# Squares of the state powers on either of two engines, and a new written-out order of 1808 steps

## The chip, the cores and the metric

One core of one Trainium2 chip runs the whole kernel. The metric is device time in microseconds (us), as the median of several executions. The core has five engines that run at the same time, each with its own queue of instructions, taken strictly in the order in which the program puts them: TensorE (PE in the profile, its weight loads PEld), VectorE (DVE), ScalarE (ACT), GpSimd (POOL) and SyncE (SP), which here issues all DMAs. An instruction that must wait for another engine's result holds up everything behind it on its own engine.

## The reference, cut to what matters

```python
a = _A_ref(x, wq, wk, wv, wo, beta)      # attention in 4 segments of 512 tokens, 32 heads of 16, with a memory
    logits = einsum('bhqd,bhkd->bhqk', qs, ks) * scale + mask ; p = softmax(logits)
    o = g * (pq @ M) / (pq @ z + 1e-6) + (1 - g) * (p @ vs)      # M, z: summed over the segments before
b = _B_ref(u, A_re, A_im, B_re, B_im, C_re, C_im, log_dt, Dskip) # state-space convolution, u = x
    P = exp(dt * A * l)                  # for all l < 2048: powers of one complex number for each (d, n)
    K = einsum('dn,dnl,dn->dl', C, P, dt * B).real
    y = irfft(rfft(u) * rfft(K))[:L] + u * Dskip
return g * a + (1 - g) * b               # g = sigmoid(x . gate_w)
```

x is 2048 x 512 in bf16. The powers exp(dt A l) are made by squaring: from Z, squared nine times, come the 1st, 2nd, 4th, ... 512th power.

## The kernel before, in words

The program is written as a graph of 1808 steps (`build_graph`). A step is one DMA, one instruction of ACT, DVE or POOL, or a group of matmuls. Its parts, with the tags used in the texts below:

- **State powers** (`ssm_prep`, `ssm_powers`; tags prep, pow, pwc; lines 840 to 866). For each half h of 256 channels x states and each k < 9: a square of Z on ACT (line 850, 128 x 512 floats, real and imaginary part at once), the difference of its halves on DVE (851), and the product 2 Re Im on DVE (852); they are the next Z. A cast of Z to bf16 (858 on ACT, 859 on DVE), a negated copy (862) and a small DMA make the form that the tables use. In `pow0.2`, 0 is the half and 2 the k.
- **Tables** (`tables`, tags tabc, tab, lag; lines 1316 to 1404). For each of four channel groups DVE multiplies powers into two tables (lines 1346, 1349, 1355, 1358); tabc are the copies of 256 elements that begin a table, either engine may do them. PE makes the convolution's kernel from the tables (lag), and an eviction brings it from PSUM.
- **Attention** (`project`, `scores`, `ophase`; tags pk, pq, sc, mk, pv, nrm, mem, oT). For each segment s and head group hg, `sc s.hg.X` are the scores on PE and then the exponential on ACT (lines 1190 and 1237, 128 x 2048), pv the product with the values, nrm the normalisation on DVE (lines 1151, 1152, 1154), oT the transposition of the result. oT3.3 is the last.
- **Convolution** (`conv`; tags X, E, K, Y, V). X, E and K are products on PE with evictions (line 229 on ACT, 230 on DVE), Y is DVE's product (1487), V the inverse product on PE, its eviction, and a DMA of 128 KB that scatters the rows of V into V2. CD is the load of the constants that K and V use.
- **Finals** (`finals`; lines 1503 to 1559). For each of 16 output blocks PE adds up: `fin` (three head groups; for blocks 8 to 15 also the skip term), `fir` (first half of V2), `fih` (the last head group, needs oT of all four segments), `fis` (second half of V2, so it needs every scatter of V16 to V31). Blocks 8 to 15 stay in PSUM ("held") and out is one eviction with a scale (232 on ACT, 233 on DVE). Blocks 0 to 7 are spilled: xD (1521) and spl (1543) on DVE before fih, out (1557) on DVE after fis.

What sets the order: `ORDER` (line 375) is a text with one word for each step, in one global order. In `1036v/0` 1036 is the number of the step in the graph, `v` puts a step that either engine may do on DVE (`a` on ACT; other steps have no letter that counts), and the numbers behind `/` are the buffers or PSUM banks that its tiles take. `replay` (in the class `Sched`) deals the words out to the engines' queues, so each engine's order is the global order cut to its own steps; `emit` puts a semaphore wait before a step for every producer, and for the last users of the buffer or bank that it takes. Nothing is decided at run time. SP's queue, which holds 257 DMAs, is such an order too: a DMA whose data is not there yet stops all DMAs behind it. `evac` (line 227 on) makes an eviction or copy that either engine may do:

```python
return self.op("ANY", 0.0, None, r=r, w=w, pw=pw, key=key,
               alts={"ACT": (("As" if sb else "A", n, scale is not None), fa),
                     "DVE": ((("V4" if sb is True else sb) if sb else "V2" if psum16 else "V1", n), fd)})
```

Of the kernel before, what the change touches and what calls it, by code (L numbers as in the profile page):

```python
# [7 lines left out]
ACT = mybir.ActivationFunctionType  # L8
# [355 lines left out]
PW, PWS = (1.0, 8.0), 0.6  # L364
# [11 lines left out]
9/0 0/0 15/0 16/0 10/1 66/0 29/0 32/0/0 38/1/0 39 33v 41/0 48/1 30/2 31a 40/2 13/2 12/3 47/3 11/4 17/3 43/4 50/5 42/6  # L376
49/7 54/0 44 3/0 51 45 46 56/8 18 19 52 53 215/0 67/4 69/5 55/9 59/0 57/10 58 34/0/1 61/11 70v/0 60/12 64/0 68v 62/13
71/0 72/1 27/0 14/5 36/6/2 74a/0 73 75 24/0 218/1 63 23/0 266/2/0/0 35a 186/2 220/0 85/3 83/1 84 1236/1 26/0 222/7 37a
189/2 7/0 76 1244/5/0 181/4 1249/4/1 77/3 95/0 22/0 199/0 78/5 96/6 97 103/1 626/0 182/3 86v/1 1/0 184/0 841/0 79 221a
87 88 106a/2 1242/0 219a 1243a 1245a 104/7 105 115/1 185/0 206/6 107 117/0 91/1 2/0 116 207/0 1246 118a/3 210/1/1/1  # L380
211a 187/0 212 129/4 1247/0 65 6/0 108 20 127/1 200 128 119 190 1248a 399/0 5/0 183 267a 1036v/0 98v/4 142v/5 213/1/0
141/6 214a 120 21 139/1 223a 228/0/0/0 1252/2/0 201 229 627/5 628 208/0 1253a 1257/0 140 1040v/0 1039v 1250a 216/3
217a 224 268 1044 225 1037v 1251 1038v 230 842/1 843 130v/6 271/2/1/1 413/1 256/0/0 1042/0 257 1045 151/2 152/7 1254/3
131 1041 153 132 258 231 311/0/2/2 143 1043 89/3 272 233/0/1 234 165/2 227 188 235 1255a 226 154v/7 269/1/1 238/0/2
239 1049 166v/8 312a 144 202/0 1050 270a 155 90 8/0 1237/3/1 156 1046 273 236/0 240 1239/1 1240a 237 241 99/1 1238a
1256 167 242/0/3 168 203/0 243 244 274 1051 1263/2/0 1264a 1047/0 1052 1265/1 101/3 1266a 163/2 357/3/2 287/0/1 288
1053 245 209/0 1048 100 246 1241 416/2 1278/1 289 417a 247/1 1056/0 358a 232/1/0 275 1054 276/0 250/0/3 251 252 400/2
401 1268/3/1 248 164 1270/1 249/0 175a/9 314/2/0 315a 253/0 254 1269a 283/0/3 284 1061 255 259 1055 1271a 1267 4/0 285
1260/2/0 1261a 1272 1258/3 176 177 1057 1259a 278/0/2 279 280 1062 1262 260 261/2 1273/1/1 1275/2 1276a 313 354/3/3/1
355a 316/2/0/0 1274a 1277 1063 301/0/0 1058 262 302 317 1059/0 281/3 263 264 303 403/0 1286/1/0 1287a 282 286 290 402  # L390
291 359/0/1/1 1060 360 319 318 1065 1066/0 295/0/2 292/3 1294/2/1 1295a 296 297 28/0 1067 320/1 361 1296/2 362 363
1068 1069/0 338/0/1 339 1299/0 293 1064 191/0 109/0 1070 1297a 364 1298 192/0 340 1071/2/0 1075/1 1076 1077 204 111/4
110 121/3 294/1 1079/0 1080 1081a 123/0 1072 1078a 205 1073 1074a 1083/0 1086v/0 1088a 1284/3 1285a 1090v/0 122 298/0
356 1087v 299 300 1094 1092/0 1089v 1095 136a/4 330/0/2 331 332 1085 135/6 112v/2 1091 304 1288 133/1 1279/1/1 472/2/1
473a 113 114 1093 305 321/0/3 1099 306/4 1084 1096 322 323 134 145/2 1100 1097/0 1082 405/3/1/0 406a 341/2 342 307
344/0/0 345 1281/3 346 1101 1280a 476/0 308 309 1098 1282a 1283 1102 420/0 1106/0 421a 326/0/1 327 426/1/0/0 146/7 328
1103 1307/3/0 427 1308a 147 157/0 324/0 325 366/0/3 367 368 343 1105 428 408/3/0 1104 80a/0 329 1107 333 334 335/5
1108 375/0/1 376 347 160a/3 377 348 1109/0 349/0 418/1 371/0/2 372 419a 409a 1111 124a/1 373 1110 469/1/0/2 1302/3/1
412/1 470a 383/0/0 384 1303a 1115 336 1116/0 369/1 370 374 337/0 81 125 385 1117 126 1112 1300/0 1301a 265/0 1305/3
1306a 378 379 389/0/3 137 390 158/2 159 386/0 82 1118 350 1119/0 380/1 1304 351 352 414/3 404/1 387 391 102v/6 161  # L400
477/2/1/1 92a/5 407 431/0/1 432 415a 381 388 423 425 422 172a/8 1113 382/1 392 393 1309 1120 1114 162 433 93 645/3/0
424 471 478 440/0/0 441 394/2 646a 479 429 94 1121/1/0 171/3 1129/3 1122 169/3 1123 277 395 1130 442 138 1125/2 1131a
353 148a/9 1126 1127 365 448/0/2 396 1128a 449 480 450 430/0/1 1312/3/1 173 1313a 1124a 174 1140v/0 481 1136v/0
522/2/2/1 1144 1138v 170 1145 1137v 1139v 454/0/3 523a 434/3 1149 1142/0 482 455 456 149 150 576/0/2 1133 1310/1 451/2
178a/7 452 1135 435 1141 1311a 1314 577a 436/0/2 437 438 647/1 1150 648a 1143 1151 1147/0 1146 410/0 1289/0/0 1290a
489/0/1 490 1152 1148 179 180 439 453 310 1317/1/1 1291/0 1155 491 493/0/2 1336/0 494 1292a 1156/0 1315/0 1318a 1153
495 457 458 1316a 397 690/1/3/0 691a 484/0/3 485 1157 1348/1 1154 486 1159/0 1132 1134 525/0/0 526a 1158 1161 411
459/3 443 530/1/0/0 444 445/4 531 1160 532 501/0/0 446 502 503 487/0 1166/0 1165 1340/2 488 492 524 1337/1/0 1167 1341
447/0 507/0/3 1397/3 1162 508 1168 474/1 1342a 460 1163 504/3 505 506 573/1/1/2 461 1169/0 496 1164 509 552/0/0 553
574a 581/1/1/1 497 510 554 511 635/2/1 844 1293 1319 1321/0 1345/1 1320/0 1350/4/0 636a 1170 462/3/5/0 512/0 398 498/1  # L410
845 1171/5/0 463 582 637/0 1175/2 1176 1351a 1177 1178a 1172 1173 513 464 583 514/1 475 1333/2 1174a 1324/4 533 465
1334/1/1 1335a 515/1/2/1 499 558/0/1 640 527/1 575 516 559 1401/0 560 529/1 517 500 195/0 1179/1 1180 629 1322/0/2 528
1181a 518 1190v/0 1447/1 466 584 1187v/0 566/1/4/0 535/0/2 536 567 1352/2 534/1 1194 1188v 585 568 1195 569 1369/2 586
1199 1323a 537 1346/0 1347a 1186v 555/2 519 544/0/3 1189a 545 546 643/3 1200 538/1 1191 467 644a 1185 539 1201 520
521/0 1192/0 630 1202 556 698/0/0/0 699 540/0/2 541 542 1193 700 1197/0 744/3/0 745a 1196 1326/0 1203 578/1 593/0/0
594 595 1183 1327a 741/3/0/1 1198 742a 557 543 1204 605/0/2 606 1419/1 196 607 1206/0 561 562 1338/0 563/3 1339a 564
468 1182 1394/0 1349/3/1 1353 1354a 1355 588/0/1 589 1205 641/0 565/0 547 590 642a 608/3 609 1211 580/0 548 549/0
597/0/2 598 599 1028/0 591/2 1207 1212 1325/0/2 1184 1328/1 1329 610 1330a 550 592 1343 596 1208 551 1213 611/0/3 612
613 600 632/0/2/2 633a 634 1209/0 1357/2 1398/1/3 638 1402 1403a 1409/2 614 601 602/5 1210 1216/0 663/0/1 664 1331 603
1360/4 615 570 1344 1377/1 604/1 616/1 860/0/1 862/1 1215 861a 863a 654/0/0 655 1214 1356 1410/2/4 1217 1219/0 1218  # L420
1220 856/0 1364/3 743 1413/0 693/1/2 617 1030/0 857a 656 675/0/2 1414 694a 193 618 1415v 1225/0/0 1226 1227 676 579
# [1227 lines left out]
```

## Time and profile before

| what | us |
|---|---|
| median of 3 runs | 292.19 |
| lowest, highest run | 289.70, 292.36 |
| span of the profiled execution, first to last instruction | 287.5 |
| around the span, to the median | 4.7 |

The time of the profiled execution as a run is not listed by itself; its span is what the profile measures from the first to the last instruction, so it is set beside the median and the lowest run.

How to read it. The page gives each engine's busy time and its share of the span. A row of a group is: line, engine, operation, out<-in (partitions x elements, type), number of instructions, then busy time in all, mean ns of one, idle time of the engine just in front of them, and what ended it. A row of the timeline is: start, length (both us), engine, line, operation, number of instructions merged, and in brackets the idle time before with what released it. A row by stages is: stretch, length, busy time of each engine with the number of instructions, granted clock of PE, busy share of the DMA engines, GB/s. ACT and DVE begin an instruction before the one ahead has ended, so the distance between two starts is shorter than the duration.

### The profile page before, as it was taken

Reading aid. Unit: us, or ns where it says so; the run is one execution under the profiler, and the core shown is the slowest. Engines: PE = TensorE matmul, PEld = TensorE weight load, DVE = VectorE, ACT = ScalarE, POOL = GpSimd, SP = SyncE. Lnnn points to the kernel's source line nnn. Section 1 sums busy time; section 2 is a strip of 40 time slices with the busy share of each in tenths; the row PEclk is TensorE's granted clock in tenths of the full one; section 3 lists DMA queues with packets and bytes.
Section 4 is the critical chain, followed back from the end, with each engine's and each line's share of the span. In section 5 each row is a group of like instructions: output and inputs, shape, how many; then the busy total and the mean of one; then the engine's idle time right before and its main releaser. Section 6 shows DMA issues by size and latency. Waiting matters only on the chain.

```text
span 287.5 us, 9336 instructions
## 1 busy us (share of the span) xinstructions
PE 253.1 (88%) x3896; PEld 158.7 (55%) x3947; DVE 265.0 (92%) x617; ACT 254.6 (89%) x320; POOL 5.0 (2%) x10
## 2 busy tenths in 40 slices
PE   5767888787898989979999989999999999999992
PEld 2424454564556546756766657665555454555661
DVE  3998999999999999979999999999999999997782
ACT  5998999999999999989989999999999999983212
POOL 5000000000000000000000000000000000000000
PEclk9999899999999999979999999999999999999999
DMA  6996762421125256914643388585776795894224
GB/s 164 270 223 143 184 203 84 130 87 42 41 47 134 63 141 205 226 32 97 188 132 102 90 252 244 166 232 161 234 215 168 207 229 160 243 186 102 72 109 182
DMA packets 60187, 44.49 MB, mean 155 GB/s; under 512 B 36209, under 2 KB 53490, under 8 KB 60146
## 3 DMA queue, kind: packets, MB, share of 16 engines
q1 hardware_dynamic: 60146, 43.90, 57.0%
q8 instruction: 31, 0.51, 0.8%
q14 instruction: 10, 0.08, 0.1%
HBM read 22.09 MB, written 7.86 MB: 104 GB/s over the span
## 4 chain that ended last, share of the span: by engine, by line
ACT 35%; PE 28%; DVE 26%; issue 5%; DMA 3%; SPq 0%; DVEq 0%; ACTq 0%
PE psum L706 28%; ACT sb L1237 10%; ACT sb L229 10%; ACT sb L1190 8%; DVE sb L1346 7%; DVE sb L1355 3%; ACT sb L850 3%; DVE sb L230 2%; DMA sb<-sb 2%; DVE sb L1349 2%; DVE sb L1487 2%; DVE sb L1358 2%; DVE sb L1249 1%; DVE sb L1154 1%; ACT sb L1021 1%
## 5 line engine op out<-in xcount | busy, mean ns | idle before, releaser
L706 PE MATMUL psum<-sb 128*128 128x17 bf16 (+17 forms) x3808 | 247.4, 229 | 23.5 <-ACT sb L1190 7.4
L706 PEld LDWEIGHTS psum<-sb 128*128 128x128 bf16 (+6 forms) x3859 | 153.5, 102 | 115.5 <-issue 20.7
L229 ACT ACTIVATE sb<-psum 128x512 bf16<-128x512 f32 (+4 forms) x155 | 87.7, 624 | 7.6 <-PE psum L706 6.4
L1237 ACT ACTIVATE sb<-psum 128x2048 bf16<-128x2048 f32 x40 | 76.0, 1899 | 2.1 <-PE psum L706 1.7
L1190 ACT ACTIVATE sb<-psum 128x2048 bf16<-128x2048 f32 (+1 forms) x40 | 70.1, 1751 | 2.8 <-PE psum L706 2.7
L1346 DVE TENSOR_TENSOR sb<-sb 128x4096 bf16<-128x4096 bf16 (+3 forms) x24 | 37.7, 1569 | 0.0
L230 DVE CAST sb<-psum 128x512 bf16<-128x512 f32 (+1 forms) x49 | 29.9, 626 | 1.1 <-PE psum L706 0.9
L1355 DVE TENSOR_TENSOR sb<-sb 128x512 bf16<-128x512 bf16 (+1 forms) x48 | 25.0, 537 | 0.1
L1249 DVE TENSOR_TENSOR sb<-sb 128x1024 bf16<-128x1024 bf16 (+1 forms) x40 | 22.6, 577 | 0.2
L1487 DVE TENSOR_TENSOR sb<-sb 128x1024 bf16<-128x1024 bf16 x32 | 21.6, 685 | 0.9 <-ACT sb L229 0.5
L1349 DVE TENSOR_TENSOR sb<-sb 128x2048 bf16<-128x2048 bf16 (+3 forms) x24 | 20.7, 861 | 0.0
L232 ACT ACTIVATE sb<-psum,sb 128x512 bf16<-128x512 f32 x6 | 4.0, 687 | 12.3 <-PE psum L706 12.3
L1154 DVE TENSOR_TENSOR sb<-psum,sb 128x256 bf16<-128x256 f32 x32 | 13.3, 417 | 0.3
L1358 DVE TENSOR_TENSOR sb<-sb 128x512 bf16<-128x512 bf16 (+1 forms) x24 | 12.9, 536 | 0.0
L850 ACT ACTIVATE sb<-sb 128x512 f32<-128x512 f32 x18 | 11.8, 660 | 0.0
L1151 DVE RECIPROCAL sb<-psum 128x16 f32<-128x16 f32 x32 | 7.9, 252 | 1.8 <-PE psum L706 1.7
L1291 DVE TENSOR_TENSOR sb<-psum,sb 128x512 bf16<-128x512 f32 x12 | 8.2, 687 | 0.2
L858 ACT ACTIVATE sb<-sb 128x512 bf16<-128x512 f32 x12 | 8.0, 683 | 0.0
L1072 ACT ACTIVATE sb<-sb 128x512 bf16<-128x512 bf16 x12 | 8.0, 663 | 0.0
L1021 ACT ACTIVATE sb<-psum 128x512 bf16<-128x512 bf16 x12 | 7.8, 646 | 0.0
L852 DVE SCALAR_TENSOR_TENSOR sb<-sb 128x256 f32<-128x256 f32 x18 | 7.5, 424 | 0.0
L851 DVE TENSOR_TENSOR sb<-sb 128x256 f32<-128x256 f32 x18 | 7.5, 423 | 0.0
(78 smaller groups left out, 122.3 us busy)
## 6 DMA issues: line engine op xcount, KB each, us to landing
sb<-sb SPq DMA_DIRECT2D x64, 128.0 KB, 3.2
sb<-c_DN SPq DMA_DIRECT2D x32, 224.0 KB, 3.0
scr_Z<-sb SPq DMA_DIRECT2D x16, 256.0 KB, 3.2
sb<-scr_Z SPq DMA_DIRECT2D x16, 256.0 KB, 3.6
sb<-in_A_x_dram SPq DMA_DIRECT2D x5, 512.0 KB, 4.6
sb<-c_DN SPq DMA_DIRECT2D x16, 160.0 KB, 3.3
out_dram<-sb SPq DMA_DIRECT2D x8, 256.0 KB, 2.1
scr_O<-sb SPq DMA_DIRECT2D x12, 128.0 KB, 2.7
```

The costliest lines, as they stand in the source:

```text
L229: fa = lambda e: e.activation(dst(), src(), ACT.Copy)
L230: fd = lambda e: e.tensor_copy(dst(), src())
L706: mm = lambda e, o_, l, r_, st, sp, **kw: e.matmul(o_, lhsT=l, rhs=r_, start=st, stop=sp, skip_group_check=True, **kw)
L850: op("ACT", ("As", 512), lambda e, sq=sq, Z=Z: e.activation(ap(sq, n=512), ap(Z, n=512), ACT.Square), r=[Z], w=[sq], key=PW[h] + PWS * k)
L1190: o = op("ACT", ("Ax", 4 * n), lambda e: e.activation(ap(pT, dims=[[512, 4], [1, n]]), ap(P, dims=[[512, 4], [1, n]]), ACT.Exp, scale=0.25 ...
L1237: o = op("ACT", ("Ax", 2048), lambda e, P=P, pT=pT: e.activation(ap(pT, n=2048), ap(P, n=2048), ACT.Exp, scale=0.25), r=[P], w=[pT])
L1249: op("DVE", ("V2", 128 * nb), lambda e, pT=pT, dims=dims: e.tensor_tensor(ap(pT, dims=dims + [[1, 128]]), ap(pT, dims=dims + [[1, 128]]), ...
L1346: op("DVE", ("V2n1" if n == 1 else "V2", 512 * n), lambda e: e.tensor_tensor(ap(tile, 2 * dst, [[2 * (sp - dst), 2], [2 * ne, 128], [1, 2 ...
L1349: op("DVE", ("V2n1" if n == 1 else "V2", 256 * n), lambda e: e.tensor_tensor(D_(), D_(), ap(tile, 2 * sp + ne * 128, [[-ne * 128, 2], [2 * ...
L1355: op("DVE", ("V2x" if sstep > 2 else "V2", 256 * n), lambda e, half=half: e.tensor_tensor(run(t2, n, 0, 1) if half else run(tile, ne, dst, ...
L1358: op("DVE", ("V2", 256 * n), lambda e: e.tensor_tensor(D_(), D_(), ap(t2, n * 128, [[-n * 128, 2], [2 * n, 64], [1, 2 * n]]), ALU.add), r= ...
L1487: op("DVE", ("V2", 1024), lambda e, Y=Y, XAB=XAB, K3=K3, Ke=Ke, xo=xo, u=u: e.tensor_tensor(ap(Y, dims=[[512, 2], [1, 512]]), ap(XAB, xo, ...
```

## The change

The square of line 850 may now be done by ACT or by DVE (there as a product of Z with itself), as the letter in `ORDER` says:

```diff
@@ ssm_powers
-                    op("ACT", ("As", 512), lambda e, sq=sq, Z=Z: e.activation(ap(sq, n=512), ap(Z, n=512), ACT.Square), r=[Z], w=[sq], key=PW[h] + PWS * k)
+                    op("ANY", 0, None, r=[Z], w=[sq], alts={
+                        "ACT": (("As", 512), lambda e, sq=sq, Z=Z: e.activation(ap(sq, n=512), ap(Z, n=512), ACT.Square)),
+                        "DVE": (("V1", 512), lambda e, sq=sq, Z=Z: e.tensor_tensor(ap(sq, n=512), ap(Z, n=512), ap(Z, n=512), ALU.mult))})
```

`ORDER` is replaced as a whole. It has the same 1808 steps. The mean distance between a step's old and new place is 16 places. Its first lines:

```diff
-9/0 0/0 15/0 16/0 10/1 66/0 29/0 32/0/0 38/1/0 39 33v 41/0 48/1 30/2 31a 40/2 13/2 12/3 47/3 11/4 17/3 43/4 50/5 42/6
...
+16/0 15/0 38/4/0 39 9/0 0/0 10/1 66/0 32/7/0 30/0 203/0 33v 41/0 48/1 31a 17/3 67/0 40/2 26/0 69/1 49/3 47/4 43/5 44
+215/0 11/2 29/0 50/6 45 51 46 7/0 12/3 52 42/7 34/2/1 54/0 53 18 56/8 55/9 57/10 68v/0 59/0 58 61/11 24/0 1236/1 62/12
...
```

Which engine does what is changed for 21 steps. Of the squares, 95 (pow0.2) goes from ACT to DVE; the other 17 have the letter a and stay. Of the other steps that either engine may do:

| from DVE to ACT | from ACT to DVE |
|---|---|
| 1036, 1038, 1040 (tabc0), 1086 (tabc1), 1187 (tabc3): copies of 256 | 74 (pwc0.0): cast of 512; 1088 (tabc1), 1189 (tabc3): copies of 256 |
| 1541 (K9, 256), 1632 (K22), 1695 (K31): evictions | 1228 (lag3, 480), 1544 (V9), 1677 (V28), 1684 (V29), 1698 (V31): evictions |
| 1773 (out9) | 1779 (out10), 1784 (out11), 1795 (out13) |

Places that the texts below use, in each engine's own queue:

- SP, start, before: 9 (parameters), 0 (identity), 15 (log dt), 10, 66 (x), 13 and 12 (parameters), ..., 24 (wv) as twelfth. After: 15, 9, 0, 10, 66, 26, 11, 7, 12, 24 as tenth, 1236 (x again), 27, 13, 14.
- ACT, start, before: pow0.1, an eviction, pow1.0, pow0.2, a gate, pow0.3. After: pow0.1, then nine other instructions, pow0.3.
- DVE, end, before: 1016 (mask of sc3.3.B1), 1019 to 1021 (nrm3.3.1), Y29, 1006 and 1007 (nrm3.3.0), Y30, 1008 (nrm3.3.0), xD3, spl3, 1027 (oT3.3). After: Y31, xD3, a mask, xD2, Y29, Y30, 1007, 1016, 1008, V31, V29, 1019 to 1021, spl7, 1027, spl3, spl2, spl0, out11, out10.
- PE, end: behind 1026 (oT3.3) stood 48 steps, now 51; before fis11, the first fis, now come fir11, fin2, fir0, fin10, fir2, fin8, fih11, fih3, fih14, fir10, fir8, fir5, fih10. K31 (1694) stood behind sc3.3.B0 (997) and now stands ahead of it.
- SP, end: the scatter 1664 of V26 stood ahead of those of V25, V29 and V30, and is now behind V25, an input load, V28, V27, V29, V30, V31 and another input load.

More of the change, by code (lines that the diff above doesn't have):

```diff
@@ L381 @@
[L381 to L420, printed above, removed]
@@ new lines @@
+288 416/2/1 168 1048 358a 400/0 28/0 1267 289 209/0 1053 100 232/3/0 246 275 1054 190 1056/0 276/0 109a/3 165 1055
+250/0/3 251 1270/3/1 247/1 417a 314/2/0 401 252 253/0 254 315a 1271a 175a/9 403/0 283/0/3 1057 1061 8/0 1278/1 1268/2
+1269a 284 1260/3/0 1258/2 255 248 285 278/0/2 176 1259a 279 1261a 1062 249/0 1272 1275/2/1 259 280 260 1273/3 1276a
+354/1/3/1 301/0/0 1274a 177 1063 316/2/0/0 281/3 1058 302 1059/0 282 355a 261/2 317 1060 359/1/1/1 1262 318 286
+1294/2/0 1066/0 290 262 319 1277 263 264 303 295/0/2 1286/0/1 360 111/1 1065 1295a 362 1287a 1067 296 320/2 291 361
@@ L465 @@
+1761/5 1722 1753/2 1769/4 1802/7 1743 1723 1737/5 1801v 1803 1705/3 1734/1 1770 1754 1804 1762 1735 1733/1 1731 1805
+1755 1785 1771 1736 1806a 1763 1772 1773a 1706 1791/0 1744/7 1807 1792 1745/2 1774 1738 1786/2 1787 1714 1788 1789/0
+1793 1707 1746 1794 1739 1715 1790a 1747 1795v 1796
 """
```

127 lines of the change are left out of this document (79 added, 48 removed).

## The prediction

> **What bounds the kernel now.** I read the page's busy times first, then the busy time of each engine stage by stage, then the chain that ended last. The page:
>
> ```profile
> span 287.5 us, 9336 instructions
> PE 253.1 (88%) x3896; PEld 158.7 (55%) x3947; DVE 265.0 (92%) x617; ACT 254.6 (89%) x320; POOL 5.0 (2%) x10
> ```
>
> Three engines stand at 88 to 92%, so no one of them is "the" bound, and shares over the span don't say where a change of order counts. The stages do (columns: stretch, its length, then busy time of PE, PEld, DVE, ACT, POOL, granted clock, DMA share, GB/s):
>
> ```profile
> 0.00:27.00 27.00, 17.98 (x154) 9.39 (x157) 20.98 (x64) 22.30 (x44) 3.69 (x8) 1.00 0.91 206
> 27.00:126.00 99.00, 83.36 (x1718) 55.20 (x1738) 96.91 (x228) 97.27 (x129) 0.66 (x1) 0.98 0.44 118
> 126.00:250.00 124.00, 119.80 (x1778) 74.81 (x1793) 120.58 (x284) 120.52 (x131) 0.66 (x1) 0.99 0.65 179
> 250.00:258.00 8.00, 7.80 (x74) 4.27 (x76) 7.86 (x14) 7.30 (x7) 0.00 (x0) 1.00 0.95 207
> 258.00:266.00 8.00, 7.93 (x92) 4.81 (x90) 6.01 (x14) 2.54 (x5) 0.00 (x0) 1.00 0.45 109
> 266.00:283.00 17.00, 16.17 (x100) 10.21 (x99) 12.69 (x19) 4.63 (x7) 0.00 (x0) 1.00 0.36 128
> ```
>
> Read it as four stages. Up to 27 us (start) nobody is full: DVE is idle for 27.00 - 20.98 = 6.0 us and ACT for 4.7. From 27 to 250 us DVE idles 2.1 + 3.4 = 5.5 us and ACT 1.7 + 3.5 = 5.2 of 223: both are full, and a new order can win back a few microseconds there, while it can lose any number. From 250 to 258 us PE and DVE are full and ACT runs dry. After 258 us PE is the full one (7.93 of 8). The chain of work that ended last agrees for its end:
>
> ```profile
> 275.77 6.53 PE psum L706 x35
> 282.30 0.02 issue
> 282.32 0.69 ACT sb L232
> ```
>
> The last engine work ends at 283.0; 4.5 us of the span follow (the last store and the end of the program).
>
> **The change part by part.** The diff lets each of 18 squares run on either engine, but in its new order only one does: 95 (pow0.2) carries a v. The other 17 stay on ACT. So this is a change of order with 21 instructions on the other engine. The prices on ACT (count | busy, mean ns):
>
> ```profile
> L229 ACT ACTIVATE sb<-psum 128x512 bf16<-128x512 f32 x135 | 78.0, 628 | 7.3 <-PE psum L706 6.0 <-DMA scr_Z<-sb 1.1
> ...
> L850 ACT ACTIVATE sb<-sb 128x512 f32<-128x512 f32 x18 | 11.8, 660 | 0.0
> ...
> L229 ACT ACTIVATE sb<-sb 128x256 bf16<-128x256 bf16 x2 | 1.0, 506 | 0.0
> ```
>
> and on DVE:
>
> ```profile
> L230 DVE CAST sb<-psum 128x512 bf16<-128x512 f32 x38 | 25.5, 686 | 1.1 <-PE psum L706 0.9
> L1487 DVE TENSOR_TENSOR sb<-sb 128x1024 bf16<-128x1024 bf16 x32 | 21.6, 685 | 0.9 <-ACT sb L229 0.5
> ...
> L1521 DVE SCALAR_TENSOR_TENSOR sb<-sb 128x512 f32<-128x512 bf16 x8 | 5.8, 746 | 0.0
> ...
> L230 DVE COPY sb<-sb 128x256 bf16<-128x256 bf16 x18 | 4.6, 294 | 2.7 <-DMA sb<-sb 1.6 <-PE psum L706 1.1
> L230 DVE CAST sb<-psum 128x256 bf16<-128x256 f32 x11 | 4.5, 418 | 0.0
> ...
> L859 DVE CAST sb<-sb 128x512 bf16<-128x512 f32 x8 | 3.3, 425 | 0.0
> ...
> L878 DVE TENSOR_TENSOR sb<-sb 128x512 f32<-128x512 f32 x2 | 1.4, 688 | 0.0
> ```
>
> No square on DVE is in this trace. Bounds: 0.425 us (the cast with one input, L859) and 0.746 us (L1521, two inputs and a scalar). I take 0.688, L878: the same two float inputs, output and size. On ACT it takes less than its 0.66, since the next instruction starts before it ends:
>
> ```profile
> 11.99 0.62 ACT L850 ACTIVATE sb<-sb 128x512 f32<-128x512 f32 x1
> 12.51 1.00 ACT L229 ACTIVATE sb<-psum 128x1024 bf16<-128x1024 bf16 x1
> ```
>
> That is 0.52 a square. So moving it costs DVE 0.69 and frees ACT of 0.52.
>
> *Load before the tail.* To DVE go the square (0.688), the cast of pwc0.0 (0.425), two table copies (1088, 1189: 0.588) and the evictions of lag3 (480 wide), V9 and V28 (3 x 0.686 = 2.058): 3.76. Away from it go five table copies (1036, 1038, 1040, 1086, 1187: 1.470), K9 (0.418), K22 and K31 (1.372): 3.26. Net +0.5 us on DVE; on ACT the same instructions nearly cancel (five copies at 0.506 and three evictions in, seven instructions out). The load hardly moves.
>
> *Tail, step by step.* What ends last before the output is the last normalisation (nrm3.3.1, op 1021), then PE's transposition oT3.3 (1026), its eviction (1027), and all the steps fih, fis and out. DVE before:
>
> ```profile
> 259.37 0.69 DVE L1249 TENSOR_TENSOR sb<-sb 128x1024 bf16<-128x1024 bf16 x1
> 261.38 0.26 DVE L1151 RECIPROCAL sb<-psum 128x16 f32<-128x16 f32 x1 [1.33 <-PE psum L706]
> 261.67 0.18 DVE L1152 TENSOR_TENSOR sb<-sb 128x16 f32<-128x16 f32 x1
> 261.89 0.42 DVE L1154 TENSOR_TENSOR sb<-psum,sb 128x256 bf16<-128x256 f32 x1
> ```
>
> The mask multiply 1016 ends at 260.06, PE needs 1.33 us for the products that follow, and 1021 ends at 262.31. In the new order these stand ahead of 1021 in addition: the 3.76 above, the evictions V31 and V29 (2 x 0.686), xD2 and xD3 (2 x 0.746), Y29 and Y30 (2 x 0.685), and the three instructions of nrm3.3.0 (0.26 + 0.18 + 0.42): 8.85. Gone from ahead of it: the 3.26 above and spl7 (0.75, priced as L1521): 4.01. Net +4.84. Of these 1.79 (V31, V29 and the last of nrm3.3.0) stand between 1016 and 1021 and fill the wait of 1.33. So 1021 ends at 262.31 + 4.84 - 1.33 = 265.8 instead of 262.3. That is nearly free: before, oT3.3 was late for another reason, its place in PE's order and nrm3.3.0, which then came last. Its eviction:
>
> ```profile
> 266.70 0.69 DVE L230 CAST sb<-psum 128x512 bf16<-128x512 f32 x1 [0.42 <-PE psum L706]
> ```
>
> The transposition ended at 266.7, so it began at about 266.1 (0.6 for four transposes of two inputs, an estimate from the 128-wide price below, with the fill). New: 265.9. That is 0.2 earlier. Behind oT3.3, PE has fin10, fin2 and four fir more, fin11, fin14 and one fir14 fewer; that is 10 matmuls of 512 columns against 7, and 4 of 128 against 8:
>
> ```profile
> L706 PE MATMUL psum<-sb 128*128 128x512 bf16 x82 | 19.1, 380 | 0.1
> L706 PE MATMUL psum<-sb 128*128 128x128 bf16 x36 | 3.4, 225 | 0.0
> ```
>
> These rows are for 262 us to the end. The means overlap, so I divide time by work: 20.3 us up to 282.3 over 82 + 36/4 = 91 wide units is 0.223 each, hence 3 x 0.223 - 4 x 0.056 = +0.45. PE then ends at 282.3 - 0.2 + 0.45 = 282.6. DVE: the eviction of oT3.3 ends at about 267.3, three spl follow until 269.6, and out11 waits for fis11, which PE reaches at 265.9 + 5.3 = 271.2 and ends at 271.4 (before it the transposition, ten steps of one matmul at 0.223, fin2 with 3, and fin10 and fin8 at 0.89 each). Behind out11 stand 15 more of about 0.75, since four of the eight held outputs are now DVE's (before: two); 16 x 0.746 = 11.9 gives 283.3, against 283.0. I take +0.3 for the tail.
>
> *SP's queue in the tail.* The price of an issue, and the landing (median us from issue, last column):
>
> ```profile
> 261.41 1.27 SPq L225 DMA_DIRECT2D sb<-sb  x2
> ```
>
> ```profile
> sb<-sb SPq DMA_DIRECT2D x64, 128.0 KB, 3.2
> ```
>
> The scatter of V26 (1664) is now last of its kind, behind those of V25, V28, V27, V29, V30 and V31 and two input loads, and every fis needs all of them. By the sums above V29's eviction ends at 265.8 - 0.86 = 265.0; four issues later, at 0.64 each, V26 leaves at 267.5 and lands at 270.7, half a microsecond ahead of fis11. Taken at 0; up to +2 if DVE is late.
>
> *Start.* c_ident moves from second to third among SP's issues (about 0.5 later), log_dt from third to first (1 earlier); the two inputs of the first exponent chain meet at the same time. The weights of the value projection go up two places, the third parameter pair goes down behind the second load of x. The state powers get later: pow0.2's square stands on DVE behind cb0's first product, and ACT takes pow0.3 behind nine other instructions. By their places, ACT reaches the square of pow0.5 some 3 us later than before, and covers it with evictions (xl1, tok, pk) that it did later before. ACT's load ahead of the first exponential of scores hardly changes: two table copies and one square come in, the square 95, the cast of pwc0.0, another square and a gate go out. I take 0. Bounds: -1 (a quarter of ACT's idle time there) to +3 (the delay falls on DVE in full).
>
> *Middle, 27 to 250 us.* The exponentials keep their sequence, and PE's order is nearly the old one. Around them steps are exchanged with neighbours some 16 places off in 1808. No row prices an exchange. Below, at most 5.5 us of DVE's idle time can go; half of it, -2.7, is my end. Above, a wait hurts only where an engine's supply was just in time; PE's idle time in these stages, 15.6 + 4.2 us, is the nearest row for how much cover PE's results have, and I put the end at +5, a quarter of that. Between ends far apart I stay near zero, at +0.5, since there is less idle time to win than to lose.
>
> Sum: 0 (start) + 0.5 (middle, with the load in it) + 0.3 (tail) + 0 (SP) = +0.8 on a span of 287.5. The profiled span lies 4.7 below the median of 292.19 and 2.2 below the fastest run, 289.7; I set the difference on the median: 293.0.
>
> **Rivals.** *A: the state powers starve DVE (slower).* DVE's next link, pow0.5's difference (128), waits for ACT's square; between it and the link before stand only cb0's 183, two short ones, pk0.0's mask and one power product, about 1.4 us. If ACT comes 3 us later and the tables behind (lines 1346 to 1358) wait for it, DVE's 5.5 us of slack are gone from the start, and the sum gets +3.5: 295.7. It decides from a delay of about 1.4 us on. Against it: much of DVE's other work (cb, gates) was moved into this place.
>
> *B: V26's scatter or V29's eviction holds the tail (slower).* If DVE reaches 1021 more than 1 us later than I reckon, fis11 waits on the queue, and each microsecond delays PE, which has little else left: +3, 295.2.
>
> *C: the new order closes idle time (faster).* K31's five matmuls of 512 columns (5 x 0.223) now stand ahead of the third last scores, 1.1 us of PE work less behind 250 us. With PE full from there, that is -1.1 if DVE keeps up, and half the middle's idle time is another -2.7: 288.4. For it: after 250 us PE is idle only 0.2 and 0.1 us of 8, and in the 17 us row 0.8, nearly all behind its last matmul at 282.3. Against it: DVE carries 4.84 us more ahead of 1021. By the Trainium skill, page "Perfetto Trace Analysis", section "Identifying the Most-Contended Engine", matmul busy time is a poor measure of how near PE is to its limit, and the busy time of LDWEIGHTS is to be used. By it (4.27 of 8, 4.81 of 8, 10.21 of 17) PE has room after 250 us, K31's earlier place would bring nothing, and C would end at 289.5. The rows of time against work, 0.223 us for each 512 columns without a gap, speak for PE as the limit there.
>
> That the square itself matters is no rival: 0.17 us of difference cannot be seen.
>
> **How the numbers follow.** A measurement of this kernel can tell about 1%, 2.9 us, from no change (the three runs alone spread over 2.7). My forecast, within that, 0.46, its own range 290.5 to 295.1; A 0.20, B 0.14, C 0.20. So faster 0.20, same 0.46, slower 0.34. The range goes from C's end, 288.5, to A and B with a middle that loses too, 298.
>
> **What would show it.** Right: the first exponential of scores at 27 to 28 us; DVE's idle time between 27 and 250 near 5.5; 1021 ending at about 266; PE full until 282 to 284, and the last eviction on DVE, not ACT. A: DVE idle before 45 us behind L850. B: PE idle in front of the first fis behind a DMA of sb<-sb. C: ACT and DVE idle by less than 3 us in the middle. Wrong altogether: many small waits of PE, DVE and ACT on each other, each under 1 us, that add up to over 3 us.

## The result, and the profile after

| | before | after |
|---|---|---|
| median, us | 289.94 (20 runs, 287.19 to 292.36) | 291.74 (20 runs, 288.98 to 296.46) |
| profiled execution: run time, span, us | 289.70, 287.5 | 290.78, 288.6 |
| engine work ends at, us | 283.0 | 284.2 |

The ratio is 1.0065, 95% interval 1.0039 to 1.0092: slightly slower, and within the 1% that the prediction called no change. Both profiled executions have 2.2 us around the span. The median of 292.19 that the prediction started from was of three runs and lay 0.8% above the median of 20.

Here is the page after (its first lines of busy time and the row on the landing of the scatters), and then the stages with the same columns as before:

```profile
span 288.6 us, 9394 instructions
PE 258.8 (90%) x3947; PEld 157.8 (55%) x3947; DVE 266.6 (92%) x620; ACT 252.8 (88%) x317; POOL 5.0 (2%) x10
...
sb<-sb SPq DMA_DIRECT2D x64, 128.0 KB, 4.1
```

```profile
0.00:27.00 27.00, 18.93 (x159) 9.96 (x160) 22.11 (x67) 22.63 (x44) 3.72 (x8) 0.97 0.82 198
27.00:126.00 99.00, 86.92 (x1772) 55.63 (x1768) 97.76 (x228) 97.88 (x130) 0.65 (x1) 0.99 0.45 115
126.00:250.00 124.00, 119.54 (x1745) 71.93 (x1744) 116.96 (x276) 118.77 (x131) 0.65 (x1) 1.00 0.73 186
250.00:258.00 8.00, 8.00 (x100) 4.50 (x99) 7.96 (x16) 7.45 (x8) 0.00 (x0) 1.00 0.69 191
258.00:266.00 8.00, 8.00 (x78) 5.03 (x77) 7.35 (x18) 3.44 (x4) 0.00 (x0) 1.00 0.12 41
```

Read it by stage again. From 27 to 126 us DVE and ACT are idle less (1.2 and 1.1 us against 2.1 and 1.7), from 126 to 250 us more (7.0 and 5.2 against 3.4 and 3.5). The DMA share of that stage went from 0.65 to 0.73, and a scatter lands 4.1 us after its issue (median) instead of 3.2. The chain ends on DVE, no longer on ACT:

```profile
249.29 34.11 PE psum L706 x287
283.40 0.02 issue
283.43 0.75 DVE sb L233
```

Where the time went is best seen by one kind of step in both traces. Below, *lead* is the start of an exponential of scores against the same step in the profile of before (us; negative is earlier). The heads are the time of that step before, in us; the last column is PE's last fis. The numbers are read off the timelines; the rows of the experiments are explained further down.

| | 27.4 | 116.3 | 132.9 | 159.3 | 187.6 | 194.5 | 216.9 | 243.3 | 256.3 | fis |
|---|---|---|---|---|---|---|---|---|---|---|
| after | -0.6 | -0.4 | -2.6 | -2.2 | -2.2 | -0.5 | +0.1 | +1.6 | +1.6 | +1.1 |
| e1_square_back | -0.9 | -0.5 | -2.9 | -2.5 | -2.5 | -1.5 | -1.0 | +0.4 | +0.4 | -0.1 |
| e2_letters_only | +1.4 | +1.8 | +0.2 | +0.5 | +0.7 | +0.7 | +2.3 | +2.6 | +2.6 | +7.3 |
| e3_head_new | 0.0 | +0.4 | -1.7 | +2.0 | +2.4 | +2.5 | +2.5 | +2.5 | +2.5 | +2.5 |
| e4_tail_new | -0.2 | +0.4 | -0.4 | +2.5 | +2.4 | +4.8 | +5.4 | +6.8 | +7.6 | +7.1 |
| e5_head_even_cut | -0.5 | +1.3 | -0.6 | -0.2 | +4.9 | +4.9 | +4.9 | +4.9 | +4.9 | +4.9 |
| e6_tail_even_cut | -0.9 | -0.9 | -2.8 | -2.8 | +4.2 | +7.0 | +8.2 | +9.6 | +10.7 | +10.1 |
| e7_last_45_old | -0.7 | +1.3 | -1.1 | -0.7 | -0.8 | 0.0 | +1.1 | +8.0 | +8.0 | +8.0 |
| e8_middle_only | -0.5 | -0.8 | -3.0 | -2.6 | +1.4 | +1.4 | +1.4 | +1.4 | +1.5 | +1.5 |
| e9_store_earlier | -1.4 | -1.1 | -2.9 | -2.5 | -2.6 | -1.0 | -0.5 | +1.3 | +1.3 | +0.8 |
| e10_middle_load_earlier | -0.3 | +1.0 | -0.9 | -0.6 | +2.0 | +2.0 | +2.0 | +2.0 | +2.0 | +2.0 |
| e11_square_alone | 0.0 | +1.0 | -0.6 | -0.5 | -0.4 | -0.4 | -0.4 | -0.2 | -0.2 | -0.2 |
| e12_slack_transfers_moved | +0.2 | +0.7 | -1.6 | -1.2 | -1.0 | -0.4 | +4.2 | +5.7 | +6.1 | +5.6 |

Two things stand out in the first row. The first is that the 2.2 us won between 116 and 133 us are mostly not the new order's: e11, with the order of before, makes up 1.6 us in the same place. The profile of before lost them there, to TensorE's clock (stretch, length, PE, PEld, DVE, ACT, POOL, granted clock, DMA share, GB/s; before, then e11):

```profile
123.00:126.40 3.40, 1.74 (x43) 1.32 (x37) 2.33 (x9) 2.61 (x4) 0.00 (x0) 1.00 0.03 7
126.40:129.80 3.40, 3.40 (x42) 2.69 (x41) 3.02 (x10) 2.83 (x3) 0.00 (x0) 0.50 0.23 51
129.80:133.20 3.40, 3.29 (x75) 2.43 (x75) 3.19 (x7) 3.21 (x5) 0.00 (x0) 1.00 0.23 53
```

```profile
123.00:126.40 3.40, 2.62 (x63) 1.73 (x64) 3.02 (x13) 3.39 (x6) 0.00 (x0) 1.00 0.11 34
126.40:129.80 3.40, 3.06 (x48) 2.13 (x47) 3.40 (x11) 3.16 (x5) 0.00 (x0) 1.00 0.23 51
```

In before PE was busy for half of a stretch and then ran at half clock (0.50) for 3.4 us. So for a comparison of the two orders some 1.6 us are to be added to the lead behind 133 us: at 256 us the new order is about 3.2 us late, not 1.6. The second thing is where that loss lies: behind 187 us, 1.7 us at 187 to 194 and then four steps of 0.5 to 0.7 between 204 and 241 us. The largest wait is DVE's, for a store:

```profile
190.85 0.42 DVE L1156 TENSOR_TENSOR sb<-psum,sb 128x256 bf16<-128x256 f32 x1 [1.97 <-DMA scr_O<-sb]
```

### The profile page after: what moved, and what is told of

It reads as the page before. It is cut to its first block, busy times and chain, and to the rows that moved or that the text cites. A ratio compares the mean times of both kernels' runs of the same rounds, so it can differ in the third digit from the quotient of the medians.

```text
span 288.6 us, 9394 instructions
## 1 busy us (share of the span) xinstructions
PE 258.8 (90%) x3947; PEld 157.8 (55%) x3947; DVE 266.6 (92%) x620; ACT 252.8 (88%) x317; POOL 5.0 (2%) x10
## 4 chain that ended last, share of the span: by engine, by line
ACT 32%; PE 31%; DVE 14%; DMA 11%; SPq 6%; issue 3%; DVEq 0%
PE psum L706 31%; ACT sb L1192 14%; ACT sb L229 11%; SPq L225 6%; DMA sb<-c_DN 6%; DVE sb L1348 3%; DMA sb<-in_B_C_im_dram 2%; ACT sb L860 2%; DMA sb<-sb 2%; ACT sb L851 2%; DMA scr_O<-sb 2%; DVE sb L1351 1%; DVE sb L1357 1%; DVE sb L230 1%; ACT sb L1239 1%
## 5 line engine op out<-in xcount | busy, mean ns | idle before, releaser
L706 PE MATMUL psum<-sb 128*128 128x17 bf16 (+18 forms) x3859 | 252.7, 230 | 21.0 <-ACT sb L1192 9.2
L229 ACT ACTIVATE sb<-psum 128x512 bf16<-128x512 f32 (+4 forms) x153 | 86.7, 613 | 8.3 <-PE psum L706 5.4
L230 DVE CAST sb<-psum 128x512 bf16<-128x512 f32 (+2 forms) x51 | 31.6, 633 | 2.8 <-PE psum L706 2.2
L1351 DVE TENSOR_TENSOR sb<-sb 128x2048 bf16<-128x2048 bf16 (+3 forms) x24 | 20.6, 858 | 0.0
L232 ACT ACTIVATE sb<-psum,sb 128x512 bf16<-128x512 f32 x4 | 2.6, 686 | 17.0 <-PE psum L706 17.0
```

The source lines that it names most:

```text
L229: fa = lambda e: e.activation(dst(), src(), ACT.Copy)
L230: fd = lambda e: e.tensor_copy(dst(), src())
L706: mm = lambda e, o_, l, r_, st, sp, **kw: e.matmul(o_, lhsT=l, rhs=r_, start=st, stop=sp, skip_group_check=True, **kw)
L1351: op("DVE", ("V2n1" if n == 1 else "V2", 256 * n), lambda e: e.tensor_tensor(D_(), D_(), ap(tile, 2 * sp + ne * 128, [[-ne * 128, 2], [2 * ...
```

## The experiments

The theory at the start was the prediction's own: the square is free, and what is lost is lost where order and supply no longer fit. Its rival was A, the powers late at the start. As the runs came in, the theory had to be changed twice; the runs stand here in the order in which they decide.

**The square put back.** One letter of the changed kernel:

```diff
-95v/2
+95a/2
```

> The changed kernel with one letter undone: square 95 (pow0.2) is on ACT again, everything else as in the change. Theory (the change is its order, the square is worth 0.17 us of load): within 1 us of the changed kernel, so a ratio to before of 1.003 to 1.010, first exponential of scores at 26.5 to 27 us. Rival A (the state powers, put back by the square on DVE, starve DVE): 2 us or more below the changed kernel, ratio under 1.000.

Ratio 1.0121, interval 1.0066 to 1.0176; median 291.2. Rival A falls: the lead is within 0.3 us of the changed kernel's until 187 us. The end of the profiled execution is better by 1.2 us, in part since the wait for the store is 1.3 us instead of 2.0. The ratio of six runs all the same stands higher, above the 1.003 to 1.010 that were expected, though its interval reaches into them; that execution, 289.65 us, was the fastest of the six. One profile and one ratio of six runs can differ here by half a per cent either way, so below the profiles are used for where time is lost, the ratios only where they are far apart.

**The square alone.** The order of before, one letter:

```diff
-95a/0
+95v/0
```

> The kernel before, its order unchanged, with a single letter changed: the square of pow0.3 (step 95) runs on DVE instead of ACT. Theory of the prediction (the square costs 0.69 us on DVE and 0.52 on ACT, and the loads of the state tables at the start hide what it delays): ratio 0.997 to 1.003, first exponential within 0.7 us of before. Rival (the 1.4 us that the run e2_letters_only lost by its first exponential is this letter's: ACT waits at each step of the chain of powers for DVE, where the square stands behind other work): first exponential 1 to 2 us late, ACT waiting 0.9 us or more at pow0.1 or pow0.3, ratio 1.004 to 1.009, unless the lag is taken back later.

1.0020, interval 0.9984 to 1.0057, and the first exponential at the same 27.4 us. ACT does wait, 0.95 us, in front of pow0.3, and the first exponential is not late for it. The prediction's price of the square holds, in the old order too:

```profile
L851 ACT ACTIVATE sb<-sb 128x512 f32<-128x512 f32 x17 | 11.3, 667 | 0.9 <-DVE sb L854 0.9
...
L852 DVE TENSOR_TENSOR sb<-sb 128x512 f32<-128x512 f32 x1 | 0.7, 683 | 0.0
```

**All 21 letters, the order of before.**

```diff
-74a/0 ... 95a/0 ... 1684a ... 1773v ... 1779a ... 1784a ... 1795a
+74v/0 ... 95v/0 ... 1684v ... 1773a ... 1779v ... 1784v ... 1795v
```

> The order and all buffers of before; only the 21 letters of the change (square 95 and 20 movable steps on the other engine). Theory (load is nearly even, order is what counts): ratio 0.997 to 1.004. Rival (the evictions V28, V29, V31 and four held outputs on DVE are what makes the end later): the same end as the change, ratio 1.006 or more, with the last eviction on DVE after 284 us.

Missed: 1.0254, interval 1.0203 to 1.0304. Of the 7.3 us, 1.4 are lost by the first exponential, 2.1 at 197 to 222 us, and 4.7 behind the last one (the 1.6 us of the old profile's half clock go the other way). PE in its tail:

```profile
261.77 1.82 PE L706 MATMUL psum<-sb 128*128 128x512 bf16 x36
264.79 11.29 PE L706 MATMUL psum<-sb 128*128 128x17 bf16 x72 [1.20 <-DVE sb L1251]
277.28 1.04 PE L706 MATMUL psum<-sb 128*128 128x512 bf16 x4 [1.20 <-DMA sb<-sb]
```

```profile
265.60:269.00 3.40, 3.40 (x10) 1.23 (x9) 1.60 (x6) 0.45 (x1) 0.00 (x0) 0.50 0.77 175
```

PE waits for DVE, which has more to do there, runs at half clock for 3.4 us (the row by stretches), and then waits for the last scatter in front of the fis: the mechanism of rival B. So the letters cost several microseconds in the old places, and the new order takes most of that back; by which of its moves, no run shows. The 1.4 us at the start are not the square's alone, as e11 lost none of them; but with the other letters ACT waits 2.1 us in front of the squares, against 0.9 in e11.

**Halves of the two orders.** If the loss sits in one half, the other half alone should be free of it. `|` is the seam:

```diff
# e3: new order up to the seam, then that of before
+... 579 1415v | 1447/2 196 468 1343 ...
# e4: before up to the seam, then new
+... 656 675/0/2 | 631/0 1389/2 692 1414 ...
```

> The first 980 words of the new order (to about 155 us), then the remaining 828 steps in the order of before, with the letters of before; 21 tiles take another buffer or bank than in before. In the trace of the change the exponentials of scores run 2.2 us ahead of before from 130 to 190 us, and that lead is lost later. Theory (the lead is won in the first part of the order and lost in the rest of the new order): the lead stays, 2 us below before, ratio 0.990 to 0.996. Rival (the end is set by PE or DVE whatever comes before, so that a lead is used up): ratio 0.998 to 1.003.

> The first 980 words of the order of before, then the remaining steps in the new order with the new letters; 18 tiles take another buffer or bank. Theory (the rest of the new order loses what the first part won): the change without its lead, 3 to 4 us above before, ratio 1.009 to 1.015. Rival (the end is set by PE's last 34 us whatever comes before): as the change, ratio 1.003 to 1.008.

e3: 1.016 (1.0109 to 1.0211); e4: 1.0259 (1.0198 to 1.032). Both missed, and both for the seam itself: the lead jumps there by 3.5 and 2.7 us. Half clock stands right behind both seams, 6.83 us of it in e3 and 3.41 us in e4, which is 3.4 and 1.7 us of work. Two rows of the table say more than that. Behind the seam e3, in the order of before, stays at +2.5 to the last column: a lag is neither added to nor regained. e4, in the new order, goes on losing, 5 us from 187 to 256 us. So I looked for a seam at which both orders have done the same work on PE, ACT and DVE to 0.4 us.

```diff
# e5: new up to the seam, then before
+... 771/0/1 1447/2 | 468 1343 1030/0 572 ...
# e6: before up to the seam, then new
+... 1234 771/0/1 | 1476/1 1232 1233 1490/2 ...
# e7: new up to the seam at 235 us, then before
+... 1614v 1638/0/0 | 926 1594 892 1639v ...
# e8: before up to the first seam, new up to the seam of e5, then before
+... 1345/1 1320/0 | 640 195/0 ... 771/0/1 1447/1 | 468 1343 1030/0 572 ...
```

> As the earlier kernel with the new head, but cut behind word 1050 (about 165 us), where both orders have done the same work to within 0.4 us on each engine; behind it the order and letters of before. Theory (the lead of 2.2 us is won in the new head; the earlier cut lost 3 us at its seam, behind which steps of both orders piled up): no jump at the seam, exponentials of scores 2 to 2.5 us ahead of before to the end, ratio 0.990 to 0.996. Rival (a lead at 165 us is used up later, since the order of before behind it meets the same DMAs): exponentials level with before at 250 us, ratio 0.998 to 1.003.

> The order and letters of before up to the same even cut (word 1050), behind it the new order and letters. Theory (the new order behind 165 us loses 3 to 4 us by itself): exponentials of scores 3 to 5 us behind before at 256 us, ratio 1.009 to 1.016. Rival (the loss is only the using up of a lead): less than 1.5 us behind, ratio 0.998 to 1.005.

> The new order up to word 1520 (about 235 us, another even cut), then the order and letters of before for the last 45 us: the evictions V28, V29 and V31 and the held outputs 10, 11 and 13 are on ACT again, V26's scatter is early again. Theory as in the prediction (the new tail costs 0.3 us, the rest lies before it): within 0.7 us of the change. Rival B (V26's scatter, the evictions on DVE): 1.5 us or more below the change, ratio under 1.002.

> Before up to word 750 (about 117 us), the new order from there to word 1050 (about 165 us), then before: both cuts even to 0.4 us. In the trace of the change 1.9 us of the lead come between 117 and 133 us, around the third lag evictions. Theory (the middle alone wins that): exponentials 1.5 to 2 us ahead from 135 us on, ratio 0.992 to 0.997. Rival (the win needs the new start before it): no lead, ratio 0.998 to 1.004.

Measured: e5 1.0109 (1.0057 to 1.0161), e6 1.038 (1.032 to 1.0439), e7 1.0241 (1.0183 to 1.03), e8 1.0104 (1.007 to 1.0138). All four jump 5 to 15 us behind the seam, by 4.5, 6.8, 4.5 and 3.9 us, though the cut was even. What was not even is SP's queue. PE in the four (e5, e6, e7, e8), each row with the wait in front of it:

```profile
175.03 1.13 PE L706 MATMUL psum<-sb 128*128 128x256 bf16 x6 [2.86 <-DMA sb<-c_DN]
```

```profile
179.78 1.37 PE L706 MATMUL psum<-sb 128*128 128x512 bf16 x31 [4.22 <-DMA sb<-scr_Z]
```

```profile
242.91 1.46 PE L706 MATMUL psum<-sb 128*128 128x512 bf16 x3 [2.31 <-DMA sb<-c_DN]
```

```profile
171.95 1.29 PE L706 MATMUL psum<-sb 128*128 128x256 bf16 x21 [2.23 <-DMA sb<-c_DN]
```

In each, PE waited for one load. That wait is only a half or so of the jump. The rest is the clock, here in e8:

```profile
169.00:172.40 3.40, 1.17 (x13) 0.79 (x10) 1.97 (x4) 1.99 (x2) 0.00 (x0) 1.00 0.96 277
172.40:175.80 3.40, 3.40 (x35) 2.15 (x33) 2.94 (x7) 1.44 (x3) 0.00 (x0) 0.50 0.52 166
175.80:179.20 3.40, 3.40 (x41) 2.31 (x39) 2.04 (x8) 3.31 (x5) 0.00 (x0) 1.00 0.34 94
```

A wait of 2.2 us, and then 3.4 us at half clock, which is 1.7 us of work: 3.9, the jump. For e5 the same sum is 2.86 + 1.7 = 4.6 against 4.5, for e7 2.31 + 1.7 = 4.0 against 4.5, and for e6, with 6.83 us of half clock, 4.22 + 3.4 = 7.6 against 6.8. These four kernels therefore can't show which part of the new order is good; they show what one late load costs. e6 adds that the order of before can be 2.8 us ahead of its own profile at 133 us, which confirms that this lead is not the new order's.

**The load at e8's seam sent earlier.** The load of CD4 stood in SP's queue behind two scatters:

```diff
-1480/3/1 846/1 710 1405 801 800 ... 1404 1498/0/2 ... 1493/2 1504/0 1505/3/0
+1480/3/1 1504/0 846/1 710 1405 801 800 ... 1404 1498/0/2 ... 1493/2 1505/3/0
```

> The kernel of the run e8_middle_only with one step moved: the load of CD4 (step 1504) goes ahead of the two scatters of X13 in SP's queue, directly behind V0's matmuls that free its buffer. There it would be issued near 167 us instead of 169.0 and land near 170 instead of 171.9. Theory (the jump of 3.9 us behind the seam is one late transfer: the cut was even for PE, ACT and DVE, but not for SP): K4's matmul starts about 2 us sooner after the seam, DVE's wait of 1.86 us and ACT's of 2.73 us there fall to below 1 us, the jump to 1.5 to 2.5 us, and the ratio by 0.005 to 0.008, from 1.0104 to 1.002 to 1.006. Rival (the two orders do not fit together at the seam in several places, and the load is one of them): another wait of 1 us or more stands there, the jump is still 3 us or more, and the ratio 1.008 or more.

1.0095 (1.0058 to 1.0132). The jump is 2.6 us instead of 4.0 between 159.3 and 187.6 us, and the way it got smaller is not the one I expected:

```profile
173.58 1.07 PE L706 MATMUL psum<-sb 128*128 128x256 bf16 x20 [1.78 <-DMA sb<-c_DN]
```

PE still waits for 1.8 us instead of 2.2: the load left only 1.3 us behind V0's matmuls, since SP was still busy with the transposed loads and a store ahead of it (one transposed load holds SP for 1.2 us). What went is the half clock; the granted clock stays 1.00 behind this wait. That is the larger part of the gain, and the edit did not aim at it. The ratio, forecast at 1.002 to 1.006, doesn't tell e10 from e8. So a late load is shown as a part of the jump; the sizes were missed.

**The store of the changed kernel sent earlier.**

```diff
-... 1423a 1411/3 1370/2 814/0/0 ... 763/0/3 796 688 1595/3 739 1440/1 ...
+... 1423a 1411/3 688 1370/2 814/0/0 ... 763/0/3 796 1595/3 739 1440/1 ...
```

> The changed kernel with one step moved: the store of oT2.0 (step 688, its data ready at 182.0 us in the changed kernel's profile) goes ahead of the load of Zx4 in SP's queue, where it would be issued near 182.2 us instead of 185.8 and land near 186 instead of 190.8. No instruction of PE, ACT or DVE is moved. Theory (what the new order loses after 187 us begins with SP's queue, which holds this store behind seven transfers that are less urgent): the 1.97 us wait of nrm2.3.0 on DVE is gone, ACT's 1.31 at K17 and PE's 1.46 at mem2.3 shrink with it, the exponentials between 197 and 219 us start 1.2 to 2.0 us sooner against the profile of before than they do in the changed kernel (-1.7 to -2.5 instead of -0.5), and if nothing takes the gain back the ratio to before falls by 0.004 to 0.007 from 1.0065, to 0.998 to 1.003. Rival (the wait was only where a lag came to light that the full engines behind it have anyway): the wait goes, the lead at 219 us is within 0.5 us of the changed kernel's and the ratio stays at 1.004 to 1.010.

The rival holds, though the ratio lies above what either side expected. nrm2.3.0 no longer waits, and DVE's next instruction waits in its place:

```profile
188.44 0.42 DVE L1156 TENSOR_TENSOR sb<-psum,sb 128x256 bf16<-128x256 f32 x1
190.05 0.69 DVE L230 CAST sb<-psum 128x512 bf16<-128x512 f32 x1 [1.19 <-DMA sb<-sb]
```

That is V10's eviction, which waits for a scatter; K17 on PE then waits 1.15 us, by the profile for DVE, while its load of constants landed at 191.36, only 0.13 us before it began. The lead falls from -2.6 to -1.0 as it did before; the ratio of six runs is 1.0143 (1.0095 to 1.0191), not better. So it was not one transfer's place. The stretch from 188 to 194 us in before, after, and e9:

```profile
188.00:194.00 6.00, 5.95 (x77) 4.12 (x77) 5.86 (x17) 6.00 (x9) 0.00 (x0) 1.00 0.88 236
```

```profile
188.00:194.00 6.00, 4.49 (x56) 2.41 (x55) 4.00 (x13) 4.52 (x8) 0.00 (x0) 1.00 1.03 267
```

```profile
188.00:194.00 6.00, 4.64 (x56) 2.51 (x55) 4.12 (x12) 4.52 (x7) 0.00 (x0) 1.00 1.04 256
```

The DMA share is 1.03 and 1.04 (the measure can go a little over 1): the transfer engines are full, transfers land 4.3 to 6.2 us after their issue, and whoever is next in line waits. The theory became: the new order crowds the transfers.

**Transfers with slack sent elsewhere.** Five DMAs of the changed kernel that are read late, two sent 17 to 23 us earlier, three 7 to 9 us later:

```diff
-... 666 571 1360/2 1476/0 ... 1518/3 572 1546/2 ... 733 468 1405 ... 739 1440/1 1372a ... 704 1417 775/0/2 ... 770/2 1416 774 ... 1380 1381 740 ...
+... 666 571 1360/2 468 572 1476/0 ... 1518/3 1546/2 ... 733 1405 ... 739 1372a ... 704 775/0/2 ... 770/2 774 ... 1380 1381 1440/1 1416 1417 740 ...
```

> The changed kernel with five steps of SP's queue moved, and no instruction of PE, ACT or DVE: the two transposed loads oT1.0 (step 468) and oT1.2 (step 572), which are read only after 250 us, go from 177.4 and 173.7 us to ahead of CD0 near 153 to 156 us, and the load of Zx11 and the two scatters of X15, which are read 9 to 13 us after they land, go from 188 to 191 us to behind the scatters of X9 near 196 us. Theory (what the changed order loses between 187 and 194 us is not one store's place but the transfer engines, whose share is 1.03 of the stretch from 188 to 194 us against 0.88 before, so that transfers land 5 us after their issue and V10, K17 and nrm2.3.0 wait together): the share of 188 to 194 us falls to 0.9 or less, the transfers issued at 185 to 188 us land 3 to 4 us after their issue, PE's, ACT's and DVE's waits of over 1 us there are gone, and the lead over the profile of before stays at -1.8 to -2.5 us until 200 us (-0.5 in the changed kernel); the ratio falls to 0.998 to 1.005 if the later stretches do not take it back. Rival (the transfers moved only bring the crowd to 196 to 206 us, where the share is 0.76 to 1.1 already): waits of 1 us or more stand at 196 to 207 us in place of those, the lead at 212 us is within 0.5 us of the changed kernel's +0.1, and the ratio stays at 1.005 to 1.010.

In the stretch itself the share falls to 0.70, PE's idle time from 1.5 us to 0.35, and the lead lost there from 1.7 us to 0.5.

```profile
188.00:194.00 6.00, 5.65 (x70) 3.30 (x68) 5.07 (x15) 5.59 (x9) 0.00 (x0) 1.00 0.70 195
```

This looks like the theory, and is not enough for it. e12's profile came into the stretch 1.2 us later than the changed kernel's (-1.0 against -2.2 at 187.6 us). Most of that lag, 1.1 us, stood already at 116 us, before the first moved transfer. It left the stretch level with it (-0.4 and -0.5 at 194.5 us). The store in front of nrm2.3.0 landed at 190.83 us, 5.4 us after its issue (190.75 in the changed kernel), the scatter in front of V10 at 190.58 (190.38), so DVE went on at the same moment and had only less long to wait:

```profile
190.93 0.42 DVE L1156 TENSOR_TENSOR sb<-psum,sb 128x256 bf16<-128x256 f32 x1 [0.90 <-DMA scr_O<-sb]
```

What the smaller crowd did change is the landing of what was issued from 188 us on: 2.7 to 3.3 us after the issue, instead of 4.9 to 5.3. The two transfers that DVE needs were issued at 185 us, ahead of it, and behind a run of transfers between tiles of SBUF, from 183 us on, that no experiment moved. So e12 doesn't show that the crowd from 188 us on costs the 1.7 us; the forecast that the lead would hold at -1.8 or better failed.

Then 4.6 us are lost between 200 and 215 us, more than the rival expected, and the ratio is 1.017 (1.0111 to 1.0229), above what either side expected. The crowd there was of issues, not of bytes (the share from 200 to 206 us is 0.77). SP's queue, then PE:

```profile
191.19 0.67 SPq L225 DMA_DIRECT2D sb<-sb  x1
194.68 0.32 SPq L225 DMA_DIRECT2D sb<-c_DN  x1
195.04 2.07 SPq L225 DMA_DIRECT2D sb<-sb  x2
197.15 0.59 SPq L225 DMA_DIRECT2D sb<-scr_Z  x1
197.78 1.10 SPq L225 DMA_DIRECT2D sb<-sb  x2
198.92 1.28 SPq L1304 DMA_TRANSPOSE sb<-scr_O  x1
200.25 1.37 SPq L225 DMA_DIRECT2D sb<-sb  x2
201.66 0.47 SPq L225 DMA_DIRECT2D sb<-scr_Z  x1
202.18 0.42 SPq L225 DMA_DIRECT2D sb<-c_DN  x1
```

```profile
206.37 2.01 PE L706 MATMUL psum<-sb 128*128 128x256 bf16 x11 [2.76 <-DMA sb<-c_DN]
```

SP stands still from 191.9 to 194.7, because the next entry, CD9, waits for its buffer, and then issues without a pause: 0.5 to 1.3 us an entry. The load of CD14 leaves at 202.2, though V13's matmuls freed its buffer at 199.9. The three moved entries, which stand ahead of it, hold SP for about 1.8 us of that. They stand behind the entry that blocks; ahead of it they would have filled SP's pause. That version was not run. No run beat the kernel before.

## Why the prediction was right, point by point

- *The level.* 293.0 against 291.74 is good in part by luck, as two errors partly cancel: the median of three was 2.25 us above that of 20, and the change was reckoned at +0.8, where the medians show +1.8. On the span, where the sum was made, +0.8 stood against +1.1, and that is luck too, as 1.6 us of the old span were the clock's.
- *The square and the load.* Right: 0.683 us on DVE against 0.688, and the square alone is not seen (1.002).
- *The start, 0.* Measured -0.6, -0.9 without the square's move; inside the bounds. The first exponential came at 26.7 us, just outside the 27 to 28 that were to show the forecast right. Rival A fell: with pow0.5's square 2.3 us later (22.9 against 20.6 us) its difference (128) is as late, but the tables that it feeds are not (tab0.3 begins at 29.7 us, before at 31.4), and DVE idles 0.4 us between 27 and 60 us.
- *The middle, +0.5.* The term that was mis-sized: from -0.6 at the first exponential to +1.6 at 256 us it is +2.2, and about +3.8 once the old profile's half clock is taken out, in the range of -2.7 to +5 that it was given. The choice near zero rested on idle time and on exchanges between neighbours on the engines. It left out that an exchange on SP's queue changes what is in flight together: 23 transfers were issued from 176 to 191.4 us (19 before), and PE, DVE and ACT, at 94% and more of the stage, had nothing to absorb a late one with. In the prediction SP was looked at in the start and the tail, and taken at 0. That the loss is the new order's behind 187 us is shown by the table: the five kernels in the order and letters of before from there on (e3, e5, e8, e10, e11) change by 0.2 us at most between 187.6 and 256.3 us, and the six in the new order (after, e1, e4, e6, e9, e12) lose 2.9 to 7.1 us. That the 1.7 us at 187 to 194 end on transfers issued at 185 us, which land 5 us later, is shown by the waits in after, e9 and e12; what makes them land late was argued and not shown. The rest, some 2 us in four steps from 204 to 241 us, stands beside waits below 1 us (0.84 at pq3.2, 0.63 at K22, 0.54 at Y24), as the sign for "wrong altogether" said, and was not taken apart.
- *The tail, +0.3.* The mask 1016 ends at 263.0 (263.1 by the prediction's sum) and 1021 at 266.1 (265.8):

```profile
262.36 0.68 DVE L1251 TENSOR_TENSOR sb<-sb 128x1024 bf16<-128x1024 bf16 x1
...
265.66 0.42 DVE L1156 TENSOR_TENSOR sb<-psum,sb 128x256 bf16<-128x256 f32 x1
...
267.42 0.69 DVE L230 CAST sb<-psum 128x512 bf16<-128x512 f32 x1 [0.67 <-PE psum L706]
```

  But that the times agree is luck, as the stage began 1.6 us late. From the last exponential on, DVE's extra work delayed 1021 by 3.77 - 1.62 = 2.15 us, not 3.5; oT3.3 came 0.9 us earlier once the lag is taken off, not 0.2; the PE work behind it grew by 0.4, as reckoned (0.45). The tail gained 0.4 us instead of losing 0.3. The last eviction is out13 on DVE, and ends at 284.2 (283.3).
- *Rival B.* V26's scatter leaves at 267.1 and lands at 270.8 (267.5 and 270.7 forecast), fis11 begins at 271.8: no wait, with 1.0 us to spare. Its mechanism is real and stands in e2.
- *Rival C.* DVE's idle time from 27 to 250 us rose to 8.3 us, so one half of the rival fell, and with it the forecast's own sign of near 5.5. Its other half fits: with K31 out of the way PE, full at 8.00 of 8 us from 250 us on, makes up 0.4 us of the lag; no run moved K31 alone. The page "Perfetto Trace Analysis" of the Trainium skill (section "Identifying the Most-Contended Engine") would judge PE's room by the weight loads, beside its share of the peak arithmetic; they were busy 4.50 and 5.03 of 8 us where PE never paused. As far as the weight loads go, the trace speaks against that rule in this stage.

## What to carry to other kernels

In an order written by hand, the DMA queue is an engine like the others: count what each stretch issues, how full the transfer engines are (in one stretch here a share of 0.88 went without a wait, and 1.03 with waits of up to 2 us), and what stands ahead of each load that lands just in time. Two orders don't simply join: behind six of the seven cuts tried here the time jumped, also where the compute engines stood even. A transfer with slack that stands behind an entry that blocks the queue delays what follows; ahead of it, it would fill the pause, which was not tried. Before reading a gain or a loss off two profiles, look at the granted clock stretch by stretch: one drop in one of them is as large as the effect of this whole change. And before a smaller wait is called a gain, look at whether the engine only came later to it.

## What the runs showed of the hardware

*A wait of PE can cost twice.* TensorE's granted clock drops to 0.50 for 3.4 us, or two or three times that, behind a stretch in which PE was idle for a good part. Each of the 14 traces was cut into stretches of 3.41 us that line up with its drops, from 12 us on. Behind all 12 stretches in which PE was busy for 46% or less the clock dropped; behind one only of nearly 1,000 above 73%; between these, behind 13 of some 75. So the same wait may or may not cost the extra 1.7 us, by how it falls on the stretches: 2.2 us in e8 did, 1.8 us in e10 and 2.8 us in e12 did not. The page "TensorE: Matmul & The Clock Gate" of the Trainium skill (section "What's actually happening") describes such a gate with a free-running window of 3413 ns, which agrees with the length of 3.41 us here; it says that the clock is halved after at least one idle window, and here PE was busy for 1.17 of 3.40 us (e8) and 1.74 of 3.40 us (before) ahead of a drop. Where the drops fall differs between executions: e11, one letter from before, has one at 63 us and before one at 126 us. In the 20 runs of the changed kernel the eight with a mean granted clock of 0.990 or more took 289.0 to 292.1 us, the six with 0.978 or less 292.2 to 296.5; so the clock goes with part of the spread over the runs of one kernel.

*Landing time is not a constant.* Scatters of 128 KB land in 3.2 us in the median of one order and in 4.1 us in that of the other, and in about 5 us where the DMA share is 1.
